# One attention and mixture-of-experts kernel, with the written order of its steps replaced

## The chip, the cores and the metric

The program runs on one core of a Trainium2 chip. The metric is device time in microseconds (us) of one execution. A core has TensorE (PE: matmuls, with its weight loads PEld), VectorE (DVE), ScalarE (ACT), GpSimdE (POOL) and SyncE (SP). SyncE issues nearly all DMA transfers of this kernel, one after the other, from one queue.

## The reference

```python
# clustered attention, 4 batches x 8 heads, 768 rows, 64 columns a head
q_assign = np.argmax(einsum(q_n, c_n)); k_assign = np.argmax(einsum(k_n, c_n))   # 16 clusters
mask = q_assign[:, :, :, None] == k_assign[:, :, None, :]
scores = np.where(mask, scale * q @ k.T, -1e9)
attn = softmax(scores); x = attn @ v                  # then heads side by side: (4, 768, 512)
# mixture of 4 experts over x, each a causal attention head of width 64
logits = x @ w_gate; topk = argpartition(-logits, 2)[..., :2]; w = softmax(selected logits)
for e in range(4):
    ye = softmax(causal(scale * (x @ wq[e]) @ (x @ wk[e]).T)) @ (x @ wv[e]) @ wo[e]
    out += (topk == e) * w * ye
```

## The kernel before, in words

The work is cut into 24 units: n = 0 to 15 are pairs of attention heads (called heads here), n = 16 to 23 are pairs of experts. The kernel first builds a plan: a list of 3726 steps (`op(...)`), each with an engine, a model duration, a function that issues its instructions, and the steps and buffers it depends on. Then `Plan.run` (line 278) walks a written list, `SEQ`, and calls the functions in that order. A token is the number of a step; a letter behind it (a, d, p) says that the step runs on its second engine (ScalarE, VectorE, GpSimdE). Each engine thus gets its own in-order queue, cut from this one list. `SLOT` says, also written out, which buffer of a tag (`ps` for the PSUM banks, `vt`, `acc`, `xt` and others) each tile takes. The durations in `op` are read by a planner that is not part of the kernel; the kernel runs the written order, whatever they say.

What one head does, with the lines that matter here:

- Its k, q and v are loaded (`load`, line 498, 384 KB each) and k and q transposed on TensorE (line 516). Clusters are found (lines 540 to 595), which gives `rows`, the one-hot rows of the mask.
- `place_rows` (line 598) sends `rows` into the operand tiles: tq<-rows and tk<-rows, 96 KB each. `put` (line 611) sends the high and low halves of k and q: tk<-hi, tk<-lo, tq<-hi, tq<-lo, each as two transfers of 192 KB. The steps of the first row of a head's maxima need `need_row` (rows, k high, q high), the scores need `need_st` (all).
- TensorE computes scores for the maxima (line 1055, 24 matmuls of 384 columns a head), VectorE reduces each (line 1061, then M at line 1065), TensorE transposes the maxima (line 1076), ScalarE or VectorE negates them into `mr`, and SyncE sends that 6 KB row into the operand tile (tq<-mr, line 1089).
- TensorE computes the scores again with the maximum row as an added term (lines 1134 and 1135, or the split pair 1138 and 1143), ScalarE takes the exponential (line 1153), and TensorE multiplies by v (line 1191). Line 1134 needs the operand halves and line 1135 also the row of maxima, tq<-mr. Both are one step, except in the first two blocks of a head, where they are two (1138, 1143).
- Row sums are added up over the blocks by `sum_op` (line 373): line 375 when GpSimdE runs it, line 376 when VectorE does. They go through TensorE (line 1215), DRAM (sd, r, rd) and a broadcast load (rb<-rd), and scale the result (line 1266), which is stored (x<-xt).

The experts project x (lines 773 and 813), take maxima and scores in the same way (lines 970, 978 and 1003) and multiply by wo (line 1305). All data are float32; "f32" and "fp32r" in the rows are two ways in which TensorE reads it.

The steps of SyncE that the prediction names: 658, 1208 and 1892 are the tq<-mr of heads 3, 6 and 10; 762 and 761 are tk<-rows and tq<-rows of head 4, 774 and 775 its tq<-hi; 580 is the v load of head 3; 1324 and 1325 are the tq<-hi of head 7, 1326 its tq<-lo, 1301 its v load; 736 is the x<-xt of head 3, 903 and 904 the rd<-r and rb<-rd of head 4; 1629 is the k load of head 9.

Of the kernel before, what the change touches and what calls it, by code (L numbers as in the profile page):

```python
# [42 lines left out]
163 164 148 149 256 257 152 153 134 120 121 112 113 254 131 258 260 423 122 123 168 169 124 125 135 116 117 137 150
151 166 161 162 146 411 167 118 147 251 566 138 139 155 156 132 128 171 133 129 140 412 413 126 127 119 141 154 159
172 160 176 165 259p 170 255p 175 142 143d 306 414 415 263 281 282 264 279 280 144 177 145 416 417 420 261 419 200
201 307 277 186 195 196 424 425 278 180 181 304 428 429 273 292 293 305 426 427p 187 191 192 283 284 267 268 430 432
431p 207 567 184 202 208 568 433 203 185 262 250 434 288 289 310 311 274 197 198 182 189 183 188 275 276 205 269 270
# [12 lines left out]
772 513 514 950 656 554 951 521 522 768d 774 769p 580 775 761 657d 658 707 814 687 688 505d 543d 510d 515d 773 776  # L60
388 389 390 221 548d 520d 553 815 955 956 804 805 948 952d 971 949p 674 957 958d 708 793 777 523 556 557d 960 555
675 524 908 558 672 673 794 778 816 817 810 806 811 781 751 1125 391 953p 392 665 822 823 818 559 973 972 961 682
683 666 667 791 659 660 661 779 807 819 783 784 792 780 782 824 962 963 964 662 684 663 685 664 1116 560 561 562 393
825 677 668 679 680 669 670 671 676d 795 678 681 789 790 689 797 798 690 692 808 809 720 693 796 686 691 820 821 965
966 812 722 723 702 703 696 697 787 967 968 970 813 785 799 800 786 788 801 802 803 826 700 701 712 713 698 699 704
710 978 974 975 717 718 721 979 1121 827 828d 829 976 980 982 983 969 981 977 984 715 716 705 706 830 711 725 709d
714 719d 724 1128 1129 1126 873 853 893 831 845 1127d 1122d 1117 1118d 874 854 832 860 861 846 694 695d 726d 727 921
728 1131 1132 894 564 1123 1124p 729 730 1119 1143 1287 563 565 1120p 1144 1142 991 987 988 858 859 1007 1008 992
1028 999 993 883 884 839 840 994 1026 841 1027 843 844 1014 1029 1010 1015 1011 1133 833 834 835 1018 1019 850 1032
851 1024 1025 1134 1135 731 732 959 733 1296 1000 1033 836 837 838 842 847 997 848 849 855 985 986 852 1030 1031 998  # L70
# [11 lines left out]
903 1325 1301 904 1629 1208 1103 1106 1107d 1355 1473 1474 1465 1466p 1461 1462p 1074d 1108 1485 1486 1484 911 1349  # L82
# [12 lines left out]
1544 1658 1659 1660d 1664 1666 1391 1392d 1667 1438 1439 1446 1802 1394 1413 1414 1397d 1665 1661 1668 1115 1283  # L95
# [111 lines left out]
    vt="010101010101111011100110010101",  # L207
    mx="0110011010100101010101011001100110101010",
# [1180 lines left out]
```

## Time and profile before

| what | value |
| --- | --- |
| median of 3 runs | 709.67 us |
| the runs | 711.19, 709.67, 703.8 us |
| the profiled execution | 703.06 us |
| its span, first to last instruction | 701.3 us |
| mean granted TensorE clock in it | 0.99 |
| data moved by DMA | 90.78 MB |

The profile is of one execution, the 703.06 us one. A row of a timeline gives start and length in us, the engine, the line, what is written and read, and in brackets how long the engine stood idle before and what ended that. Rows of SyncE are marked SPq and give the time of issuing, not of the transfer itself. PEclk is the granted share of TensorE's full clock.

### The profile page before, as it was taken

Reading aid. Unit: us, or ns where it says so; the run is one execution under the profiler, and the core shown is the slowest. Engines: PE = TensorE matmul, PEld = TensorE weight load, DVE = VectorE, ACT = ScalarE, POOL = GpSimd, SP = SyncE. Lnnn points to the kernel's source line nnn. Section 1 sums busy time; section 2 is a strip of 40 time slices with the busy share of each in tenths; the row PEclk is TensorE's granted clock in tenths of the full one; section 3 lists DMA queues with packets and bytes.
Section 4 is the critical chain, followed back from the end, with each engine's and each line's share of the span. In section 5 each row is a group of like instructions: output and inputs, shape, how many; then the busy total and the mean of one; then the engine's idle time right before and its main releaser. Section 6 shows DMA issues by size and latency. Waiting matters only on the chain.

```text
span 701.3 us, 13445 instructions
## 1 busy us (share of the span) xinstructions
PE 675.0 (96%) x4817; PEld 520.0 (74%) x4817; DVE 551.1 (79%) x1210; ACT 339.9 (48%) x787; POOL 332.5 (47%) x279
## 2 busy tenths in 40 slices
PE   8899997998988998999999999999999999999998
PEld 6778676676675775766776769787987988997766
DVE  5998986796969988999998987867677758968433
ACT  5646454465453663645664752355433334313623
POOL 6695654675834445717665742218503451404300
PEclk9999999999999999999999999999999999999999
DMA  7787567677765769565868435313022111021223
GB/s 223 170 184 171 126 173 171 171 178 148 209 160 130 184 183 219 129 191 142 194 159 222 124 93 122 92 47 92 2 68 72 48 50 61 24 100 56 76 94 121
DMA packets 70734, 90.78 MB, mean 129 GB/s; under 512 B 21088, under 2 KB 60428, under 8 KB 70668
## 3 DMA queue, kind: packets, MB, share of 16 engines
q1 hardware_dynamic: 70524, 89.90, 50.0%
q8 instruction: 38, 0.62, 0.4%
q14 instruction: 28, 0.23, 0.1%
q10 hardware_dynamic: 144, 0.03, 0.0%
HBM read 36.54 MB, written 12.91 MB: 71 GB/s over the span
## 4 chain that ended last, share of the span: by engine, by line
PE 53%; DVE 5%; DMA 3%; issue 2%; SPq 1%; ACT 1%; POOL 1%; DVEq 0%; ACTq 0%
PE banks L1191 10%; PE banks L773 9%; PE banks L1003 6%; PE banks L1305 5%; PE banks L813 5%; PE banks L1055 3%; PE banks L1134 3%; PE banks L1135 3%; PE banks L970 2%; PE banks L1215 2%; SPq L358 1%; DVE wvl L376 1%; PE banks L516 1%; DVE mx L1061 1%; POOL acc L375 1%
## 5 line engine op out<-in xcount | busy, mean ns | idle before, releaser
L1061 DVE TENSOR_REDUCE mx<-banks 128x1 f32<-128x384 f32 x384 | 191.6, 549 | 34.2 <-PE banks L1055 33.4
L1135 PE MATMUL banks<-tq,tk 97*128 97x384 f32 x324 | 111.4, 344 | 9.9 <-DMA tq<-mr 9.9
L1055 PE MATMUL banks<-tk,tq 80*128 80x384 f32 x384 | 112.0, 363 | 5.9 <-DMA tk<-rows 2.0
L1134 PE MATMUL banks<-tq,tk 128*128 128x384 f32 x324 | 115.3, 356 | 0.6 <-DVE mx L1061 0.6
L1055 PEld LDWEIGHTS banks<-tk,tq 80*128 80x128 f32 x384 | 69.1, 192 | 18.7 <-issue 11.6
L1153 ACT ACTIVATE p<-banks 128x384 f32<-128x384 f32 x144 | 66.6, 498 | 30.0 <-PE banks L1135 12.5
L1135 PEld LDWEIGHTS banks<-tq,tk 97*128 97x128 f32 x324 | 62.4, 193 | 11.2 <-DMA tq<-mr 11.2
L1134 PEld LDWEIGHTS banks<-tq,tk 128*128 128x128 f32 x324 | 62.1, 192 | 9.7 <-DVE mx L1061 3.2
L375 POOL TENSOR_TENSOR acc<-acc,p 128x768 f32<-128x768 f32 x21 | 39.7, 1890 | 46.8 <-DVE acc L376 44.6
L370 ACT ACTIVATE avu<-banks 128x384 f32<-128x384 f32 x31 | 15.2, 490 | 80.0 <-PE banks L1191 77.7
L978 DVE CUSTOM_DVE_ANT_0 banks<-banks,tri 128x384 f32<-128x384 f32 (+4 forms) x96 | 45.8, 528 | 7.8 <-PE banks L970 7.6
L1191 PE MATMUL banks<-p,vt 128*64 128x384 f32 x288 | 50.5, 490 | 0.0
L1153 ACT ACTIVATE xl<-banks 128x384 f32<-128x384 f32 x88 | 41.8, 497 | 14.0 <-PE banks L1135 13.3
L1153 ACT ACTIVATE xh<-banks 128x384 f32<-128x384 f32 x80 | 38.3, 499 | 16.7 <-PE banks L1135 15.7
L375 POOL TENSOR_TENSOR lo<-xk,hi 128x384 fp32r<-128x384 f32 x27 | 27.0, 1010 | 36.2 <-DVE mx L1061 12.7
L1003 PE MATMUL banks<-tk 64*128 64x384 f32 (+2 forms) x432 | 44.1, 313 | 0.0
L1191 PEld LDWEIGHTS banks<-p,vt 128*64 128x64 f32 x288 | 19.6, 137 | 24.2 <-issue 22.2
L1003 PEld LDWEIGHTS banks<-tk 64*128 64x128 f32 x432 | 34.8, 185 | 2.3 <-ACT tk L1017 0.5
L1191 PE MATMUL banks<-xl,vt 128*64 128x384 f32 x176 | 31.0, 489 | 0.0
L1266 POOL TENSOR_TENSOR xt<-avu,rb 128x384 f32<-128x384 f32 x26 | 27.2, 1055 | 7.5 <-DMA rb<-rd 6.7
L1017 ACT ACTIVATE tq<-banks 128x768 f32<-128x768 f32 (+2 forms) x41 | 26.8, 672 | 5.2 <-PE banks L1003 4.2
L1191 PE MATMUL banks<-xh,vt 128*64 128x384 f32 x160 | 28.2, 488 | 0.0
(316 smaller groups left out, 1692.6 us busy)
## 6 DMA issues: line engine op xcount, KB each, us to landing
tk<-hi SPq DMA_DIRECT2D x60, 192.0 KB
tq<-hi SPq DMA_DIRECT2D x56, 192.0 KB
rb<-rd SPq DMA_DIRECT2D x46, 192.0 KB
vt<-in_v_dram SPq DMA_DIRECT2D x16, 384.0 KB
x<-xt SPq DMA_DIRECT2D x16, 384.0 KB
kt<-in_k_dram SPq DMA_DIRECT2D x15, 384.0 KB
qt<-in_q_dram SPq DMA_DIRECT2D x15, 384.0 KB
tk<-lo SPq DMA_DIRECT2D x30, 192.0 KB
```

Of the source, the lines that this page charges most:

```text
L375: ways = [("pool", t_pool(n), lambda: POOL.tensor_tensor(dst(), a(), b(), op=fn)), ("dve", t_dve(n), lambda: DVE.tensor_tensor(dst(), a(), ...
L773: PE.matmul(m()[:, :HW], w_()[:, dc, es], x_[dc]()[:, js], start=(i == 0), stop=(i == 3 * DC - 1))
L813: PE.matmul(m()[:, :NV], x_[dc]()[:, ts], w_()[:, dc, :], start=(i == 0), stop=(i == 3 * DC - 1))
L978: DVE.tensor_tensor_reduce(ps()[:, h, :w], ps()[:, h, :w], tri[:, 512 - w:], 1.0, -3.0e38, OP.add, OP.max, to)
L1003: PE.matmul(p()[:, h, o_:HW], kone[0][r] if a is None else a()[r, ks], b()[r, qs], start=(j == 0), stop=(j == 3))
L1055: PE.matmul(ps()[:, :w], Q[0:R, 0, h, c * 128:(c + 1) * 128], K[0:R, 0, h, i * w:(i + 1) * w], start=True, stop=True)
L1061: DVE.tensor_reduce(mx()[:, h, cc, i:i + 1], ps()[:, :w], axis=AX.X, op=OP.max)
L1134: PE.matmul(p()[:, o_:HW], K[:, 1, h, ks], Q[:, 1, h, qs], start=True, stop=False)
L1135: PE.matmul(p()[:, o_:HW], K[0:R, 0, h, ks], Q[0:R, 0, h, qs], start=False, stop=True)
L1153: ACT.activation(pt()[:, h, po:po + w], p()[:, o_:HW], AF.Exp, scale=SC)
L1191: PE.matmul(av()[h * 64:(h + 1) * 64, o_:HW], d["vv"](h, kc), pt()[:, h, po:po + HW - o_], start=(kc == 0), stop=(kc == nk - 1), tile_posi ...
L1305: PE.matmul(m()[:, :n1 - n0], a_()[:, ts], w_()[:, ep, n0:n1], start=(ep == 0 and i == 0), stop=(ep == EP - 1 and i == 2))
```

## The change

The order `SEQ`, the engine letters in it and the buffer numbers `SLOT` are replaced. Steps, operations, tiles and buffers are the same 3726. The first heads follow an older order of theirs; all later steps follow an order made with a planner's model in which a transfer has an issue time, a flight time and a time for which it occupies the DMA engines, so that transfers queue one behind the other. These numbers are in the `op("sp", ...)` entries, which got a third figure. The diff, cut to the places around steps 658, 1208 and 1892 and to the changed entries:

```diff
@@ SEQ
...
-491 492 493 516 759 760 762 544 500 608 609 655 615 621 630 503 504 517 946 508 545 509 770 766 767 771 947 501 502
-772 513 514 950 656 554 951 521 522 768d 774 769p 580 775 761 657d 658 707 814 687 688 505d 543d 510d 515d 773 776
...
-1463 1364 1365 1206 1207 1366 1347 1367 1460 1468 1469 1339 1356 1340 1354 1357 1073 1464 1088 1093 1098 736 1326
-903 1325 1301 904 1629 1208 1103 1106 1107d 1355 1473 1474 1465 1466p 1461 1462p 1074d 1108 1485 1486 1484 911 1349
...
-1756d 1788 2147 2148 1789 2009 2007 1625 1890 1891 1457 2003 2029 2030 2050 2051 2143 2044 2144 2027 2028 2154 2021
-2010 1985 1892 2145 2149 2169 2152 2153 2155d 2031 2019 2020 2023 2046 2042 2043 1790 1757 1758 1791d 2157 2158 2024
...
+549 758 617 608 497 550 614 219 642 387 498 552 759 615 513 760 950 609 538 508 499 630 762 655 766 518 767 761 770
+656 946 771 657 509 658 554 768d 772 951 773 775 514 500d 519 505d 774 388 510 389 521 555d 769p 952 515 776 948d
...
+1318d 1199 1174 1177 1323p 1324 1104 1200 1192 1319p 1175 1325 1179 1083 902 1180 1198 1205 1464d 1088d 1105 1206
+1468 1207 1459 1093 1469 1208 1470 1460 1339 1374 1471d 1341 903 1329 1340 1358 1326 1473 1375 1070 1465 1342 1362
...
+1996 2009 1778 1767d 1772 1623 1624 1854 1849 1855 2007p 2003 2010 1774 1865 1779 1788 1789 1777d 1782d 1787 1755
+1756 1749 1754 1864 1866 2050 1889 1890 1891 1892 2051 2154 2155 2058 2059 1625 1626 2044 2029 2030 2048 2049 2045
...
@@ SLOT
...
-    vt="010101010101111011100110010101",
+    vt="001101010101101100011010101010",
-    acc="010101010101101010100101010101100101",
+    acc="010101010101010101010110101001101001",
...
@@ load
-            return t, op("sp", [(0.5, 4.5)], go, due, use=[t])
+            return t, op("sp", [(0.5, 2.8, 1.32)], go, due, use=[t])
@@ place_rows
-        need_row = [op("sp", [(0.6, 2.8)], place_rows(Q, 0), c2 + 8, [o_r] + free, [rows]),
+        need_row = [op("sp", [(0.6, 2.15, 0.84)], place_rows(Q, 0), c2 + 8, [o_r] + free, [rows]),
@@ put
-            return op("sp", len(pars) * [(0.65, 3.6)], go, due, after + free, use)
+            return op("sp", len(pars) * [(0.65, 2.3, 0.96)], go, due, after + free, use)
...
@@ core
-                o = op("sp", [(0.84, 1.2)], go, due + 0.5, [o] + (d["zero"] if moe else sets_free(n)), [mr, qm] if moe else [mr])
+                o = op("sp", [(0.84, 1.14, 0.04)], go, due + 0.5, [o] + (d["zero"] if moe else sets_free(n)), [mr, qm] if moe else [mr])
...
```

The number of steps on each engine, from the letters of the two lists: TensorE 1425 and 1425, SyncE 375 and 375, ScalarE 759 and 760, VectorE 915 and 871, GpSimdE 252 and 295. Of the 324 steps made by `sum_op`, 172 were on GpSimdE and 211 are now.

## Rows read from the trace of the kernel before

**Rows 1.** The page, part 1: engine busy us, share of the span, instructions.

```profile
PE 675.0 (96%) x4817; PEld 520.0 (74%) x4817; DVE 551.1 (79%) x1210; ACT 339.9 (48%) x787; POOL 332.5 (47%) x279
```

**Rows 2.** Busy us of each engine in two stretches, granted clock, DMA share, GB/s.

```profile
0.00:420.00 420.00, 397.48 (x2632) 288.84 (x2633) 358.52 (x716) 232.10 (x548) 247.64 (x191) 0.99 0.69 169
420.00:701.00 281.00, 277.54 (x2186) 231.11 (x2185) 192.56 (x495) 107.80 (x239) 84.86 (x89) 0.99 0.23 70
```

**Rows 3.** Who waited for whom, TensorE: us in total, times, longest.

```profile
PE banks L1135 <- DMA tq<-mr: 9.9, 5, 4.3
PE banks L1076 <- DVE M L1065: 2.3, 2, 2.0
PE banks L1055 <- DMA tk<-rows: 2.0, 1, 2.0
PE banks L1055 <- DMA tq<-rows: 2.0, 1, 2.0
```

**Rows 4.** Timeline of SyncE's queue, 100 to 105 us: start, us of issuing, transfer.

```profile
100.07 1.26 SPq L358 DMA_DIRECT2D tq<-hi  x2
101.38 0.59 SPq L358 DMA_DIRECT2D vt<-in_v_dram  x1
102.02 1.25 SPq L358 DMA_DIRECT2D tq<-hi  x2
103.31 0.60 SPq L358 DMA_DIRECT2D tq<-rows  x1
104.01 0.84 SPq L358 DMA_DIRECT2D tq<-mr  x1
```

**Rows 5.** Timeline of TensorE, 105 to 111 us.

```profile
105.39 0.45 PE L1134 MATMUL banks<-tq,tk 128*128 128x384 f32 x1
110.16 0.69 PE L1135 MATMUL banks<-tq,tk 97*128 97x384 f32 x1 [4.32 <-DMA tq<-mr]
```

**Rows 6.** Timeline of TensorE, three other waits for transfers.

```profile
198.77 0.60 PE L1135 MATMUL banks<-tq,tk 97*128 97x384 f32 x1 [3.28 <-DMA tq<-mr]
...
276.48 0.59 PE L1055 MATMUL banks<-tk,tq 80*128 80x384 f32 x2 [1.96 <-DMA tq<-rows]
...
309.15 0.44 PE L1135 MATMUL banks<-tq,tk 97*128 97x384 f32 x1 [1.21 <-DMA tq<-mr]
```

**Rows 7.** Timeline of SyncE's queue, the issues of those three transfers.

```profile
193.64 0.83 SPq L358 DMA_DIRECT2D tq<-mr  x1
...
270.94 0.60 SPq L358 DMA_DIRECT2D tq<-rows  x1
...
305.67 0.84 SPq L358 DMA_DIRECT2D tq<-mr  x1
```

**Rows 8.** Stretches around three waits, columns as in rows 2 (clock third from last).

```profile
110.16:113.56 3.40, 3.40 (x12) 3.21 (x13) 1.31 (x3) 1.15 (x3) 0.00 (x0) 0.50 0.31 87
113.56:117.00 3.44, 3.44 (x37) 2.43 (x36) 2.68 (x7) 2.41 (x7) 2.64 (x3) 1.00 0.93 261
198.90:202.30 3.40, 3.40 (x12) 3.31 (x13) 1.94 (x4) 0.49 (x1) 0.78 (x1) 0.50 0.97 248
277.40:280.80 3.40, 3.40 (x19) 2.34 (x21) 2.75 (x8) 1.25 (x3) 0.00 (x0) 0.50 0.36 100
```

**Rows 9.** Chain that ended last: start us, us, what (DMA from issue to landing).

```profile
249.54 1.27 PE banks L1055 x7
...
270.94 5.40 DMA tq<-rows
...
305.67 3.44 DMA tq<-mr
...
344.28 4.02 PE banks L1191 x24
```

**Rows 10.** Timelines of VectorE and GpSimdE, 407 to 409 us.

```profile
407.00 0.95 DVE L376 TENSOR_TENSOR xl<-vm,xh 128x768 fp32r<-128x768 f32 x1
...
408.72 1.73 DVE L376 TENSOR_TENSOR xl<-vm,xh 128x768 fp32r<-128x768 f32 x1
...
407.16 4.99 POOL L375 TENSOR_TENSOR acc<-acc,xl 128x768 f32<-128x768 f32 x2 [5.08 <-DVE acc L376]
```

More of the change, by code (lines that the diff above doesn't have):

```diff
@@ L43 @@
[L43 to L47, printed above, removed]
@@ L61 @@
[L61 to L65, printed above, removed]
@@ L66 @@
[L66 to L70, printed above, removed]
@@ new lines @@
+20 88 422 108 246 13 89 242 104 109 17 96 243 406 97 404 407 100 105 92 575 405 244 101 106 245 93 402p 409 111 247
+99 410 102 107 114 229 90 126 115 94 91 230p 249 86 256 95 148 252 87 168 149 163 103 421 169 157 110 257 164 152
+158 253 112 153 130 248 173 113 131 132 120 258 127 124 411 254 133 259p 128 166 260 129 155 167 125 146 398p 156
+118 412 161 147 136 226p 174 150 423 162 171 134 151 135 160 172 154 261 413 121 251 255p 137 116 414 138 304 415
+290 159 117 122 408 416 140 119 417 176 566 123 262 139 165 305 141 291 420 288 142 289 428 419 277 143 170 424 429
@@ new lines @@
+1116 520 522 957 972 822 947 787 958d 668 799 823 669 679 670 580 788 806 543 802 707 908 803 687 708 800 816 390
+659 680 810 817 660 688 665 949p 818 807 661 820 682 811 812 548 793 683 821 698 700 794 699 662 819 672 797 813 663
+673 666 553 798 717 667 804 808 701 791 805 684 718 792 795 664 955 953p 796 824 814 956 702 815 781 783 703 973 674
+782 785 809 677 779 825 678 392 960 1125 826 675 780 556 784 961 671 523 685 524d 777 557 689 778 789 558 962 690
+786 391 692 790 801 909 963 676 971 964 681 693 965 827 722 966 686 712 828d 967 829 710 968 705 696 711 969 978 706
@@ new lines @@
+833 974 979 723 559 720 975 715 970 721 867 976d 697 845 980d 716 836 855 868 704 982 837 848 560 838 878 846 856
+393 713 725 981p 983 879 709d 221 977 561 714 984 726d 834 871 835 691 1007 1117 849 1008 1028 1010 1118 839 869
+1011 872 840 562 1029 991 870 1018 719 830 841 992 995 891 1119 1019 1001 858 1002 850 859 996 1020 843 851 1021 993
+999 844 1126 994 892 860 724d 1127 831 853 832 1121 1000 1014 842 989 1122 1128 990 861 888 1296 854 1015 886 1129
+1024 1287 1123d 1003 1032 887 985 920 1124p 1030 1033 1131 1025 1142 847 1004 727 1132 694 1031 695 893 1143 889 987
@@ new lines @@
+873 988 1120p 1133 874 728d 1026 1005 1134 894 923 1012 852 863 729 1006 1144 1135 875 986 959 1027 857 1013 1136
+1022 997 1137 881 998 1138 730 883 1023 564 1139 1016 1009 876 1017 884 1292 1140 563 1034 1149 1145 1293 1141 1035
+1150 1036 882 1146 1037 877 896 1151d 1147 880d 864 1153 885d 731 1148p 1154 1152 1044 1051 890d 732 1041 1068 1052
+1155 1061 897d 895 1069 1288 1062 1045 1038 1289 1039 1130 1096 1046 1297 1040 1053 862 1097 733 1042 1294d 1189
+1290 1058 1190 1054 1077 1059 1075 1314 1172 1078 1193 1168 1043 1056 1194 1291p 1089 1173 1057 1458 1063 1090 1201
@@ new lines @@
+1635 1527 1531 1514 1241 1631 1509 1506 1528 1405 1109 1421 1507 1406 1301 1639 1515 1632 1383 1800 1384 1269 1532
+1422 1545 1380 1656 1640 1423 1546 1385 1504 1520 1518 1505 1386 1419 1521 907 1539 1381 1420 1519 1387 1398 1424
+1540 1400 1382 1274d 1395 1388 1431 1399 1529 1533 1432 1410 1530 1396 1389 1534 1512 1390 1428 1513 1391 1535 1393
+1411 1536 1392 1523 1543 1394 1110 1408 1429 1544 1541 1111 1409 1277 1655 1644 1278 1397 1401 1244 1645 1245d 1403
+910 1498 1510 1404 1525 1112 1637p 1646 1511 1524 1413 1526 1633p 1279 1647 1402 1809 921 1648 1657 1407 1499 1649
@@ new lines @@
+1697 1448 1690 1804p 1415 1815 1449d 1416 1283 1808p 1816 1701 1450 1564 1683 1684 1695 1575 1565 1568 1573 1284
+1285 1828 1827 1451 911 1980 1578 1583 1702 1685 1817 1818 1704 1679 1671 1705 1672 1819 1710 1711 1584 1585 1680
+1686 1703 1675 1594 1595 1596 1820 1821 1691 1692 1706 1714 1715 1698 1676 1699 1822 1823 1825 1824 1599 1600 1597
+1607 1687 1608 1598 1829 1830 1831 1832p 1708 1833 1834 1835 1837 1707 1452 1453 1838 1286 1673 1674 1688 1693 1614
+1712 1713 1709 1718 1604 1836 1601d 1605 1606d 1611 1612 1613 1615 1617 1618d 1616 1719 1720 1721 1983 1984 1858
@@ new lines @@
+1859 1887 1846 1875 1876 1856 1857 1847 1981 1982 1972 1973 1871 1869 1873 1872 1976 1852 1860 1870 1861 1888 1974
+1586 1977 1986 1978 1987 1454 1839 2142 1619 1456 1455 1998 1853 1979p 2151 1587d 1620d 1621 1997 1877 1878 1874
+1770 1771 1842 1740 1741 1752 1753 1883 1728 1768 1862 1863 1745 1769 1746 1881 1882 1844 1750 1751 1729 1730 1785
+1786 1884 1843 1879 1880 1840 1988 1731 1732 1841 1989 1990 1722 1723 1724 1742 1743 1733 1725 1726 1727 1759 1760
+1763 1764 1775 1737 1738 1747 1867 1735 1748 1736 1776 1975p 1999 1845 1991 1992 1850 1851 1868 1885 1761 1762 1622
@@ new lines @@
+2207 2225 2226 2485 2112 2113 2351 2327 1967 2352 926 2126 2208 2231 2196 2235 2194 2195 2197 2105 2106 2489 2101
+2102 2109 2398 2399 2115 2116 2388 2389 2206 2396 2397 2486d 2496 2497 2494 2495 2120 2353 2232 2233 2234 916 2121
+2130 2491 2487 2511 2510 2114d 930d 931 927 2119d 2124d 2129d 2490 2499 2500 912 928 2099 2657 2132 2133 2100 2134
+2156 2354 2131d 2386 2387 2236 2237 914 2296 2394 2395 2253 2400 929 2401 2501 2297 2263 2264 2248 2249 918d 2278
+2255 2241 2392 2256 2254 2250 2251 2279 2242 2666 2135 2488p 2492p 2512 2384 2244 2245 2246 2281 2282 933 936 2502
@@ new lines @@
+2775 2789 2780 2784 2785 2773 2778d 2783 2889 2890 2897 2881 2882 2978 2979 2799 2800 2843 2815 2810 2794 2795 2813
+2898 2845 2792 2793 2803 2808 2804 2483 2790 2791 3061 3062d 3063 2805 2899d 2797 2798 2802 2796d 2801d 2806 2807d
+2809 2811 2816 2814 2818 2786 2819 2787 2812d 2817d 2820 2821d 2974 2975 2968 2969 3064 3065 3066p 2951 2900 2921
+2922 2935 2936 2927 2928 2976 2977 2931 2932 2911 2912 2913 2972 2973 2905 2906 2907 2964 2965 3067 3068d 3069 2924
+2925 2919 2920 2970 2901 2966 2967 2902 2903 2971 2980 2873 3073 3074 3075 3079 2844 2653 2655 2822 2312 2823 2824
@@ new lines @@
+2981 2982 3076 3077d 3080 3081 3078 3070 3071d 3072 2983 3018 2933 2937 3019 3020 2994 2995 2996 2874 2654 2846p
+3110 3111 3002 3003 3104 3105 3010 3011 3116 3117 3007 3008 3004 3005 3102 3103 3014 3015 3016 2904 2929 2908 2909
+2988 2989 2990 2991 3114 3115 2923d 2926d 2984 3106 2985 2986 3281 2987 2825 3108 2826 3109 3181 3090 3091 3178 3182
+3179 2930d 2934d 2938d 3183 3180 3107 3172 3173 3174 3175 3176d 3177 2875 2910 2914d 3088 3089 3112 3113 3118 3190
+3186 2915 2941 2917 2916 2942 3084 3085 3119 3187 3082 3120d 2918d 2993 3086 3087 3083 3191 3092 3093 3198 3199 3192
@@ new lines @@
+3193 3006 3012 2992 3009 3013 3282 3283p 3121 3140 3141 3145 3146 3152 3153 3194 3195 3132 3133 3148 3149 3184 3185
+3196 3197 3200 3122 3123 3124 3284 3285d 3286p 3142 3143 3126 3188 3127 3128 3156 3157 2998 2939 2940 3022 3017 3021
+3024 2997 3000 3287 2656 3288d 3289 2876 2877 3278 3279d 3280 3299 3189 2828 2827d 3094 3025d 3201 3202 2999 3296
+3297d 3298 3095 3001 3290 3291d 3292 3096 2943 2944 2878 3203 2829 2879 2945 2946 3300 3023 2880 3501 3026 3293
+3294d 3295 3301 3304 3305 3326 3327 3222 3223 3330 3331 3204 3205 3206 3134 3144 3150 3147 3328 3329 3214 3215 3216
@@ new lines @@
+3224 3225 3334 3335 3230 3231 3322 3323 3227 3228 3336 3337 3208 3209 3210 3154 3211 3151d 3155 3238 3234 2947 3027
+2948 2949d 3207 3158 3332 3028 3333 3338 3159d 3239 3240 3029 3498 3324 3325 2950 3235 3236 3125 3129 3130d 3131d
+3135 3312 3313 3302 3392 3393d 3030 3031 3394 3306 3307 3308 3395 3396d 3401 3402 3397 3403 3032 3033 3398 3303 3399
+3400 3339 3310 3340 3341 3309 3138 3139d 3311 3499 3502 3162 3163d 3164 3416 3417 3213d 3412 3503p 3500p 3226 3212
+3232 3229 3410 3411 3160 3161d 3413 3136 3137 3414 3415 3360 3361 3404 3405 3362 3363 3352 3353 3418 3419 3376 3377
@@ new lines @@
+3372 3342 3373 3406 3407 3420 3233 3237 3365 3366 3346 3347 3348 3368 3507 3508 3369 3509 3408 3409 3241 3165 3504
+3505 3506p 3218 3219d 3314 3242 3097 3098 3099 3101 3038 3519 3520d 3521 3421 3513 3514 3515 3100 3166 3516 3517
+3315 3518 3422d 3423 3243d 3039 3040d 3510 3511d 3512 3217 3220 3167 3168 3244 3245d 3221 3343 3344 3542 3543 3548
+3549 3442 3443 3447 3448 3458 3459 3552 3553 3450 3451 3554 3555 3444 3445 3550 3551 3454 3455 3428 3429 3556 3557
+3430 3434 3435 3424 3425 3544 3545 3546 3370 3364 3367 3349 3169p 3316 3371d 3374 3375 3460 3431 3246 3041 3247 3248
@@ new lines @@
+3387 3388 3268 3432 3258 3259 3631 3640 3627 3641 3642 3532 3461d 3464 3465d 3433 3437 3440 3260d 3441d 3466 3269
+3643 3467 3533 3534 3589 3590 3535 3536 3356 3380 3584d 3357d 3381d 3389p 3438 3439 3592 3654 3655 3593 3594 3680
+3681 3656 3685 3686 3687 3676 3677 3261 3572 3596 3597 3321 3468 3469 3470 3682 3644 3645 3648 3649 3573 3598 3646
+3647 3650 3574 3651 3678 3566 3567 3568 3569 3570d 3585 3586 3672 3673 3571d 3575d 3587d 3591d 3595d 3599d 3669 3667
+3537 3538 3670 3274 3275 3262 3263 3276 3277 3668 3578 3602 3603d 3539 3579d 3604 3264 3265 3540 3462 3576 3675
@@ L193 @@
+3390d 3391 3474 3463d 3671d 3471 3472 3605 3473 3486 3487 3488d 3674d 3475 3476 3477 3489 3657 3600 3679d 3606 3683d
+3607 3608 3490 3491 3492 3601 3493 3577 3482 3483 3484 3485 3690 3652d 3692 3691 3653d 3660 3661 3659 3494 3495 3496
+3497 3478 3479 3480 3481 3609 3610 3662 3658d 3693 3663 3664 3611 3665 3666 3694 3684 3688 3689 3695 3696 3697 3706
+3707 3708 3709 3698 3699 3714 3715 3716 3717 3700 3701 3710 3711 3712 3713 3541 3702 3703 3704 3705 3718 3719 3720
+3721 3722 3723 3724 3725
 """
@@ L218 @@
-    ps2="31123232332231001223120300012121323203113023321103022032310322111213200032303023232010021301122331120010"
-        "32003130221303120110223003312221",
+    g="01320132",
+    ps2="32120331031231200011322313020302132310112102103223032131013300011012232210332021013033311322110332011200"
+        "31330222310333211200213011210120",
 )
@@ L602, in attention_operands @@
             free = [op("pool", 2.7, lambda: clear_rows(n % 3), t0 - 60)]
-        need_row = [op("sp", [(0.6, 2.8)], place_rows(Q, 0), c2 + 8, [o_r] + free, [rows]),
-                    op("sp", [(0.6, 2.8)], place_rows(K, 1), c2 + 8.2, [o_r] + free, [rows])]
+        need_row = [op("sp", [(0.6, 2.15, 0.84)], place_rows(Q, 0), c2 + 8, [o_r] + free, [rows]),
+                    op("sp", [(0.6, 2.15, 0.84)], place_rows(K, 1), c2 + 8.2, [o_r] + free, [rows])]
         need_row2, half_row = [], [need_row[:], need_row[:]]
@@ L669, in move @@
             def move(dst, src, due, after, use=()):
-                return op("sp", [(0.65, 2.2)], lambda: dma(dst, src()), due, after, use)
+                return op("sp", [(0.65, 2.1, 0.96)], lambda: dma(dst, src()), due, after, use)
             need_st += q_lo[::2] + [move(Q[high, 1, :, :HW], lambda: Q[low, 0, :, :HW], c2 + 14, need_row[-2:])]
@@ L1236, in go @@
                 dma(dr["s"][:, :, qd, :], ssb()[32 * qd:128:64])
-        o = op("sp", 2 * [(0.58, 1.7)], go, t1 + 7, sums, [ssb])
+        o = op("sp", 2 * [(0.58, 1.05, 0.04)], go, t1 + 7, sums, [ssb])
         r = tmp("r", (128, 12), bufs=2)
-        o = op("sp", [(0.37, 2.4)], lambda: dma(r(), dr["s"].rearrange("h f d j -> (h f d j)").rearrange("(p t) -> p t", t=12)),
+        o = op("sp", [(0.37, 1.2, 0.04)], lambda: dma(r(), dr["s"].rearrange("h f d j -> (h f d j)").rearrange("(p t) -> p t", t=12)),
                t1 + 9, [o], [r])
```

200 lines of the change are left out of this document (79 added, 121 removed), and 53 rows, old and new, of the table SEQ.

## The prediction

> **What bounds the kernel now.** I read the engine shares of the page first. TensorE shows 675.0 us of matmuls in a span of 701.3 us [rows 1], so whatever the new order gains has to come from the places where TensorE stands still or runs slowly. The two long stretches show where those are. In the first 420 us, the sixteen attention heads, TensorE is busy for 397.5 us, VectorE for 358.5 us, and the DMA engines for 0.69 of the time. In the remaining 281 us TensorE is busy for 277.5 us and DMA for only 0.23 [rows 2]. The second stretch is simply full of matmuls, and an order can't shorten it. The first has some 22 us of idle TensorE and a crowded DMA.
>
> The waits name the cause. Of the idle time before matmuls, 9.9 us in five waits is for the small transfer tq<-mr (the row of negated maxima, 6 KB) before line 1135, 2.0 us each is for tk<-rows and tq<-rows, and 2.3 us is for a VectorE reduction before line 1076 [rows 3]. A 6 KB transfer isn't slow by itself, so I looked at SyncE's queue ahead of the longest wait. From 100.07 to 104.01 us it issues four halves of tq<-hi (192 KB each), a v load (384 KB) and tq<-rows (96 KB), and only then tq<-mr [rows 4]: 4 x 192 + 384 + 96 = 1248 KB in front of 6 KB. The matmul that needs it starts at 110.16 us after 4.32 us of idling [rows 5], 6.1 us after the issue. The same shape stands before 198.77 us (idle 3.28), 276.48 us (1.96, on tq<-rows) and 309.15 us (1.21) [rows 6], whose transfers were issued at 193.64, 270.94 and 305.67 us [rows 7]. The planner's entry for this transfer was 0.84 us of issue and 1.2 us of flight, whatever lies ahead in the queue.
>
> A long wait costs a second time. From 110.16 to 113.56 us the granted clock is 0.50, the lower level (1.2 GHz), with 12 matmuls in 3.40 us against 37 in the next 3.44 us at 1.00. The same 3.40 us at 0.50 follow the waits that end at 198.9 and near 277 us [rows 8]. Each gives away 1.7 us.
>
> **The change part by part.** The edits to (issue, flight, occupancy) numbers alter nothing by themselves: the program runs the written order, and only the order, its engine letters and the buffer numbers reach the chip. All 375 SyncE steps, and all 1425 of TensorE, are the same in both. So matmul work is unchanged, and I cost three effects of the order.
>
> *Small transfers leave the crowd.* I counted, along each order, the matmul work between a transfer's place and its first user (0.18 us for a 384-column matmul, 4.0 us for a value product of six blocks, [rows 9]) and the KB issued within the 5 us ahead of it. For head 3's tq<-mr (step 658) it was 1248 KB ahead and 0 to 3.9 us of work behind; now it stands before steps 774 and 775 (the tq<-hi of head 4), with 580 KB ahead and 8.8 us behind. Head 6 (step 1208): from 2788 KB and 1.3 us to 768 KB and 2.0 us. Head 10 (step 1892): from 1920 KB and 2.4 us to nothing and 5.5 us. Head 10's last operand: from 2116 KB and 8.0 us to 576 KB and 5.6 us. Over stretches of 10 us of matmul work, six had transfers for over 300 GB/s in the old order and three have in the new. What goes, if these waits all go: 9.9 (tq<-mr) + 2.0 (tq<-rows) [rows 3] + 3 x 1.7 (clock, [rows 8]) = 17.0 us, and 1.0 of the 2.0 us on tk<-rows at the start, where the lead in the order rises from 0 to 3.5 us. Sum 18.0, bounds 12 and 20.
>
> *Other leads get shorter.* The new order starts some transfers just in time. tq<-mr of heads 4, 6 and 7 has 2.3, 2.0 and 1.5 us of work behind it with 512, 768 and 384 KB ahead. Landing took 3.44 us where 768 KB were just ahead (305.67, [rows 9]); by that I need 3.2, 3.4 and 3.0, short by 0.9, 1.4 and 1.5. Heads 13 and 14 have no work between place and user, but 4.9 to 5.2 us after the step that feeds them; SyncE often runs ahead of its place, so I take 1.5 for both together (bounds 0 and 9.4). Heads 1 and 2: 0.9. That is 6.2 us. For tq<-hi, the last operand before a head's maxima, the lead was mostly 8 to 9 us and is now 3.3 to 5.8 us in heads 1 to 10, 0.4 in head 15. A landing in the crowd took 5.40 us [rows 9] and the first half's issue 0.65 more; by that the shortfalls add up to 19.9 us at the short end of the leads and 7.8 at the long end (a 3.9 us value product may cover the place). In less crowded spots the old run did with about 4.5 us, which leaves 0 to 7.1 us; I take 1.5, near that lower row, because fewer KB now stand ahead. One wait of 2 us or more that drops the clock: 1.7. Coming back: 6.2 + 1.5 + 1.7 = 9.4, bounds 2 and 30.
>
> *Sums move from VectorE to GpSimdE.* VectorE steps fall from 915 to 871 and GpSimdE's rise from 252 to 295; 39 of these are net sums (line 376 to line 375). That takes some 40 us off VectorE in all, some 25 in the heads, where it is the second-fullest engine. TensorE waits 2.3 us for it before line 1076 [rows 3]; I take 1.0, bounds -4 and 4. If this cover fails, a GpSimdE sum of 1.8 us sits where a 0.95 us VectorE sum was, and the row sums of the head come later; nothing on TensorE's chain waits for these soon.
>
> At 407.00 us a VectorE sum takes 0.95 us and at 408.72 us the same sum takes 1.73, started while GpSimdE's pair of sums from 407.16 us ran [rows 10]. The Trainium skill (SBUF — State Buffer, "Who interferes with whom") says that a VectorE instruction with two SBUF inputs and a GpSimd instruction that reads SBUF exclude each other for a whole instruction, whichever starts first; the trace agrees, with 0.78 us added. By it more GpSimdE sums would slow the VectorE sums that remain.
>
> *The buffer numbers and the second stretch.* Which of a tag's buffers a tile takes changes everywhere, and with it what a step waits for; in the second stretch only 3.5 of 281 us are idle on TensorE [rows 2], so the most that this part can give is 3.5, and as it is reordered too it can lose as much. I take nothing for both.
>
> Sum: 18.0 + 1.0 - 9.4 = 9.6 us off the profiled execution's 703.06, or 693.5 us. The runs' median is 709.67, 6.6 above that execution. I read that spread as transfers that crowd differently from run to run; with fewer of them crowded I keep two thirds of it, 4.4 us, and forecast 698.0 us.
>
> **The rivals.** *Slower: the tight leads don't hold.* If every tq<-hi needs its crowded 6.05 us, the shortfall is 19.9 us in place of 1.5, and four waits (heads 3, 6, 9, 15) drop the clock in place of one: 5.1 us more. 693.5 + 18.4 + 5.1 = 717.0 in the terms of the profiled execution, 721.4 on the medians. For it speaks that leads fell to near half; against it that the KB issued ahead of a head's last operand in heads 1 to 10 were between 96 and 2896 and are between 576 and 1248, and that heads run at 4.5 to 5.5 us today without a wait. It decides against the change once the shortfall passes the 9.6 us gained.
>
> *No change: VectorE takes the place of the transfers.* VectorE is at 358.5 of 420 us [rows 2]. If TensorE, no longer held by transfers, is held by the maxima instead, only the clock's share comes back: 2 us, 701 and, with the full offset, 707.7. For it: the fullest stretches of VectorE; against it: its load falls.
>
> *No change: the exclusion of the sums.* If each of the 43 added GpSimdE steps held a VectorE sum for 0.78 us, VectorE would have 33.5 us more; with 61.5 us free in 420 [rows 2] I let a third of it reach TensorE, 11 us: 704.7, on the medians 709.1.
>
> **How the numbers follow.** The forecast has 0.60, VectorE's rival 0.19, the exclusion 0.05 and the tight leads 0.16. A measurement of this kernel can tell about 1% from no change. The forecast's case lies below 702.6, hence faster 0.60, same 0.24, slower 0.16. Low end: 18.0 + 4 gained and only 2 given back, 683, and a small offset, 685. High end: between forecast and the first rival, 714, where about a tenth is left above.
>
> **What would show it.** Right: the wait of line 1135 on tq<-mr falls from 9.9 to some 6 us or less, no wait of 3 us or more, one or no stretch at clock 0.50 in the heads, VectorE's busy time some 30 to 45 us lower, GpSimdE's some 50 to 80 higher, the second stretch unchanged. Wrong: waits of line 1055 on tq<-hi or tq<-rows in several heads (first rival), or unchanged attention time with waits on line 1061 (second).

## The result, and the profile after

The changed kernel takes 686.01 us (median of 4 runs, 683.79 to 688.21) where the kernel before took 706.73 us (median of its 4 runs). The ratio is 0.970, with a 95% interval of 0.963 to 0.977: faster by 3.0%. Medians here are over all runs; ratios and their intervals leave out runs more than 1.5% above the fastest of their kernel. I had forecast 698.0 us and faster; 686.0 lies in the range of 685 to 714, one us above its low end. The profiled execution of after took 683.79 us with a span of 681.9 us, that is 19.3 us less than the one of before.

The page, part 1, answers to [rows 1]:

```profile
PE 668.1 (98%) x4817; PEld 517.3 (76%) x4817; DVE 530.5 (78%) x1166; ACT 340.2 (50%) x788; POOL 391.7 (57%) x322
```

TensorE is idle for 681.9 - 668.1 = 13.8 us, where it was idle for 701.3 - 675.0 = 26.3. So 12.5 of the 19.4 us of span are idle time that went. The two stretches, as in [rows 2], show where:

```profile
0.00:420.00 420.00, 410.09 (x2747) 303.81 (x2748) 356.56 (x726) 235.39 (x558) 292.76 (x224) 1.00 0.70 176
420.00:682.00 262.00, 258.03 (x2072) 213.48 (x2071) 173.96 (x441) 104.83 (x230) 98.97 (x99) 0.99 0.20 64
```

In its first 420 us TensorE runs 2747 matmuls where it ran 2632. In the second stretch it is idle for 4.0 us, as before (3.5). The waits of TensorE, answering to [rows 3]:

```profile
PE banks L773 <- DVE mx L1061: 3.0, 1, 3.0
PE banks L1215 <- DVE acc L376: 2.4, 3, 1.5
PE banks L1215 <- DVE wvl L376: 1.4, 1, 1.4
PE banks L1321 <- DVE onesb L385: 1.1, 1, 1.1
PE banks L516 <- DMA kt<-in_k_dram: 1.0, 1, 1.0
```

The first row of before, 9.9 us on tq<-mr, has no successor: none of this view's rows names tq<-mr, tq<-rows, tk<-rows or tq<-hi. What is left at the top is VectorE's. The places where the clock fell answer to [rows 8]:

```profile
400.08:403.49 3.41, 3.19 (x10) 3.19 (x11) 2.56 (x7) 0.00 (x0) 1.51 (x2) 0.50 0.02 2
...
662.90:666.30 3.40, 3.40 (x9) 2.67 (x9) 1.43 (x7) 0.52 (x1) 0.00 (x0) 0.50 0.00 0
```

Of the three half-clock stretches in the heads none is left. One new one follows the 3.0 us wait on VectorE; the one near the end stood at 676.8 us in before too. In the new order's two later profiles the same wait was 1.4 and 3.0 us, with a stretch at 0.50 behind it each time.

### The profile page after: what moved, and what is told of

It is laid out like the page before. It is cut to its first block, busy times and chain, and to the rows that moved or that the text cites. A ratio compares the mean times of both kernels' runs of the same rounds, so it can differ in the third digit from the quotient of the medians.

```text
span 681.9 us, 13437 instructions
## 1 busy us (share of the span) xinstructions
PE 668.1 (98%) x4817; PEld 517.3 (76%) x4817; DVE 530.5 (78%) x1166; ACT 340.2 (50%) x788; POOL 391.7 (57%) x322
## 5 line engine op out<-in xcount | busy, mean ns | idle before, releaser
L1134 PE MATMUL banks<-tq,tk 128*128 128x384 f32 x324 | 113.9, 352 | 0.0
L1135 PE MATMUL banks<-tq,tk 97*128 97x384 f32 x324 | 109.8, 339 | 0.0
L375 POOL TENSOR_TENSOR acc<-acc,p 128x768 f32<-128x768 f32 (+1 forms) x26 | 45.8, 1763 | 28.8 <-DVE acc L376 27.4
L375 POOL TENSOR_TENSOR acc<-p,p 128x768 f32<-128x768 f32 x9 | 16.6, 1845 | 48.7 <-ACT p L1153 29.8
L1191 PEld LDWEIGHTS banks<-p,vt 128*64 128x64 f32 x288 | 19.4, 136 | 24.0 <-issue 20.5
L375 POOL TENSOR_TENSOR lo<-xk,hi 128x384 fp32r<-128x384 f32 x29 | 30.6, 1068 | 10.2 <-DMA tq<-lo 8.3
L1266 POOL TENSOR_TENSOR xt<-avu,rb 128x384 f32<-128x384 f32 x30 | 31.5, 1060 | 8.0 <-DMA rb<-rd 6.9
```

Source lines behind the costliest of these rows:

```text
L375: ways = [("pool", t_pool(n), lambda: POOL.tensor_tensor(dst(), a(), b(), op=fn)), ("dve", t_dve(n), lambda: DVE.tensor_tensor(dst(), a(), ...
L1134: PE.matmul(p()[:, o_:HW], K[:, 1, h, ks], Q[:, 1, h, qs], start=True, stop=False)
L1135: PE.matmul(p()[:, o_:HW], K[0:R, 0, h, ks], Q[0:R, 0, h, qs], start=False, stop=True)
L1191: PE.matmul(av()[h * 64:(h + 1) * 64, o_:HW], d["vv"](h, kc), pt()[:, h, po:po + HW - o_], start=(kc == 0), stop=(kc == nk - 1), tile_posi ...
```

## Why the tight leads hold

My fear was rows of maxima that are sent just in time. The tightest is head 7's. SyncE's queue in after, 199 to 206 us:

```profile
199.22 1.31 SPq L358 DMA_DIRECT2D tq<-hi  x2
203.90 0.83 SPq L358 DMA_DIRECT2D tq<-mr  x1
204.78 1.27 SPq L358 DMA_DIRECT2D tq<-lo  x2
```

And TensorE at the first matmul that uses it:

```profile
205.98 0.41 PE L1135 MATMUL banks<-tq,tk 97*128 97x384 f32 x1
```

Line 1135 starts 2.08 us after the issue, with no wait in brackets. SyncE had issued nothing between 200.53 and 203.90 us, and the next bulk transfer goes behind the row, not ahead of it. Head 6 is the same, with 768 KB of tq<-hi in the 5 us ahead of its row and a pause of 2.3 us between them:

```profile
174.42 2.60 SPq L358 DMA_DIRECT2D tq<-hi  x4
179.34 0.85 SPq L358 DMA_DIRECT2D tq<-mr  x1
```

```profile
181.82 0.34 PE L1135 MATMUL banks<-tq,tk 97*128 97x384 f32 x1
```

That is 2.48 us from issue to use, without a wait. In before the row of head 6 was issued at 193.64 us and waited for until 198.77, 5.13 us later [rows 6, 7]. SyncE's queue just ahead of it, in before:

```profile
188.94 1.56 SPq L358 DMA_DIRECT2D tq<-hi  x2
190.60 0.54 SPq L358 DMA_DIRECT2D vt<-in_v_dram  x1
...
192.96 0.58 SPq L358 DMA_DIRECT2D kt<-in_k_dram  x1
```

There the k load, 384 KB, is issued 0.1 us ahead of the row, with hardly a pause since the others. The bytes issued in the last 5 us are thus the wrong count: in after 384 and 768 KB of tq<-hi are among them, but they were issued before the pause. What the pauses did is in the DMA engines' share (the last column but one; it can read a little above 1). In after, behind the rows of heads 6 and 7:

```profile
180.00:182.00 2.00, 2.00 (x15) 1.11 (x14) 2.00 (x5) 0.65 (x2) 2.00 (x2) 1.00 0.06 6
204.00:206.00 2.00, 2.00 (x16) 1.82 (x14) 1.90 (x5) 1.99 (x5) 2.00 (x2) 1.00 0.01 3
```

In before, behind the row of head 6:

```profile
194.00:196.00 2.00, 1.49 (x15) 0.55 (x7) 1.97 (x6) 1.16 (x3) 0.21 (x1) 1.00 0.82 209
```

The rows of heads 6 and 7 had the DMA engines nearly to themselves. The Trainium skill (SBUF — State Buffer, "The DMA setup-cost knee") gives a transfer about 2 us that don't depend on its size; the 2.08 us from issue to use, within which head 7's row landed, agree.

## The experiments

Every kernel here computes the whole result.

**The old order with eight transfer moves** (waits of line 1135 undone where they stood):

```diff
-516 759 760 762 544 ... 769p 580 775 761 657d 658 ... 1325 1301 904 1629 1208 ... 1985 1892
+516 759 760 762 761 544 ... 769p 657d 658 774 775 ... 580 ... 1325 904 1208 1301 1629 ... 1892 1985
```

(also 1824 forward and 1296, a q load, back)

> The old order and the old engines, with the places of SyncE's transfers changed around five waits and nothing else: the rows of maxima of heads 3, 6 and 10 go ahead of bulk transfers that stood just before them, a q load goes behind the row of head 5, and the mask rows of heads 4 and 10 (tq<-rows) go to where they are ready. Theory (small transfers stuck behind bulk ones): the waits of 4.32, 3.28, 1.21, 0.9 and 1.96 us shrink to under 1 us each and at least two of the three stretches at clock 0.50 vanish, so 9 to 16 us less than before (ratio 0.977 to 0.987). Rival (the gain of the new order came from moving sums to GpSimdE): within 3 us of before. Rival (the waits just move to the next transfer, tq<-hi of the next head): within 4 us of before, with waits of line 1055 on tq<-hi of 2 us or more.

Measured: 712.34 us, ratio 0.9999 [0.9954, 1.0045]. TensorE's waits there:

```profile
PE banks L516 <- DMA qt<-in_q_dram: 5.9, 1, 5.9
...
PE banks L1135 <- DMA tq<-mr: 1.3, 2, 0.8
```

The 9.9 us on tq<-mr fell to 1.3, as wanted, but the q load that I had moved back came 5.9 us late itself. The experiment was spoilt by that move.

**The same without the q load's move:**

> The old order with the moves of the first experiment, but the q load (step 1296) left in its place, so that no bulk load comes late. Theory A (waits on the row of maxima behind bulk transfers, and their half-clock stretches, are most of the gain): line 1135 waits under 2 us in all on tq<-mr, no line-516 wait on a q load, and 8 to 13 us less than the kernel before: ratio 0.982 to 0.989, near 700 us. Theory B (the gain is spread over the whole order and a wait taken away only moves the idle time to the next late thing): ratio 0.993 or above although the waits on tq<-mr are gone.

Measured: 706.25 us against 711.27, ratio 0.991 [0.987, 0.995]: 5 to 6 us, between the two theories.

```profile
PE banks L1055 <- DMA tq<-rows: 4.2, 1, 4.2
PE banks L1055 <- DMA tk<-rows: 2.6, 1, 2.6
...
PE banks L1135 <- DMA tq<-mr: 1.3, 2, 0.9
```

The stretches at the lower level:

```profile
23.80:34.05 10.25, 10.25 (x44) 8.06 (x45) 6.34 (x15) 2.69 (x6) 6.14 (x8) 0.50 0.70 173
...
382.20:392.45 10.25, 9.52 (x49) 6.96 (x50) 4.79 (x10) 3.74 (x10) 1.96 (x2) 0.50 0.46 115
```

8.3 us of waits on tq<-mr before line 1135 went (9.9 less 1.3, and 0.3 that stand before line 1143). But TensorE, now earlier, stood 4.16 us for tq<-rows before a matmul at 382.94 us; in the kernel before it stood 1.64 us at the same place, and went on at 382.67 us. It had come there 2.25 us earlier and left 0.27 us later, and the next 10.25 us ran at 0.50, which is 5.1 us lost. The first stretch, at 23.80 us, costs as much. It follows the wait for tk<-rows, at a place that no move touched; in before's profile that wait was 2.0 us, with no stretch behind it. So this one profile, which is slower than before's, doesn't show the gain that the times show. What it does show is that freeing seven transfers isn't the change: another transfer was late next, and the new order has no wait on that one.

**The new order with bulk transfers put ahead of five rows of maxima:**

```diff
-439 315 ... 487 ... 829 ... 1469 1208 ... 1516 1379
+439 236 746 315 ... 605 751 487 ... 393 221 829 ... 1469 1326 565 1208 ... 1516 1497 1301 907 1379
```

> The new order and engines, with two or three bulk transfers (384 KB each, ready by then) put straight ahead of the row of maxima of heads 1, 2, 4, 6 and 7, which have 1.9 to 2.8 us from issue to user. Theory: each row lands 2 to 3 us later, waits of line 1135 or 1143 on tq<-mr of about 2 to 3 us come back in most of the five, and one to three stretches at clock 0.50 follow: 10 to 18 us more than the new order's 684 to 688 us, that is 695 to 705 us. Rival (sums on GpSimdE are the gain): at most 3 us more, under 691.

Measured: 694.49 us, ratio to the kernel before 0.977 [0.972, 0.981]. The new order wasn't timed beside it; in its three comparisons its medians were 685.2 to 686.0 us, 8.5 to 9.3 less, just under the 10 that I had expected at least. Of the waits

```profile
PE banks L1135 <- DMA tq<-mr: 8.1, 5, 2.6
```

this row is back. Four of the five are where loads had been put ahead, heads 1, 2, 6 and 7 (2.58, 0.95, 1.59 and 1.48 us); head 4's row, moved like them, isn't waited for. The fifth, 1.51 us at 319.62, is head 11's, where nothing was moved. The chain that ended last holds these transfers, head 11's the last:

```profile
55.24 5.09 DMA tq<-mr
84.54 3.26 DMA tq<-mr
186.75 4.19 DMA tq<-mr
213.14 3.68 DMA tq<-mr
...
313.22 6.36 DMA tq<-mr
```

With the loads right ahead a 6 KB row lands after 3.26 to 5.09 us. The KB don't fix the time: heads 1 and 2 both have 768 KB straight ahead, and took 5.09 and 3.26. Head 11's 6.36 us says more on pauses: SyncE issued nothing between 305.21 and 308.60 us, and yet the DMA engines stayed full:

```profile
306.00:308.00 2.00, 2.00 (x14) 1.96 (x13) 1.78 (x6) 2.00 (x7) 1.31 (x1) 1.00 1.07 214
```

So a pause by itself isn't enough. Another 960 KB stood straight ahead of this row too; how much of the 6.36 us comes from either wasn't separated. The place behind the bulk transfers is therefore a cause, shown from both sides. It is worth 5 to 9 us in these two experiments; how the rest of the new order's gain divides among its other moves, its letters and its buffer numbers wasn't measured.

**Order and engine letters exchanged.** The new order with the old letters (266 steps differ), and the reverse:

> The new order, with every step on the engine on which the old order had it (266 letters differ; 39 sums net go back to VectorE). Theory (transfers are the gain, VectorE is a cover): 2 to 8 us more than the new order, 688 to 695 us, with waits on VectorE and none on tq<-mr. Rival (the engines are the gain): 12 us more or above, 698 us or more.

> The old order, with every step on the engine on which the new order has it. Theory: the waits on tq<-mr stay (about 10 us in total before line 1135), so within 5 us of before either way, ratio 0.993 to 1.007. Rival (the engines are the gain): 10 us or more less than before, ratio under 0.986.

Measured: 793.35 us (ratio 1.116 [1.111, 1.121]) and 825.28 (1.159 [1.154, 1.165]). Neither expectation had the size, and the second not even the sign. The longest waits of the second are

```profile
PE banks L1076 <- DVE M L1065: 12.5, 3, 6.5
PE banks L1055 <- DVE mx L1061: 9.6, 3, 5.4
```

An engine takes its steps in the order of the list, so a step on another engine's queue stands in front of other steps than the order was made for. Order and letters can't be priced apart.

**43 of the moved sums back on VectorE** (beside a run of the new order, 685.19 us, ratio to the kernel before 0.964, as expected). The edit drops the letter that puts a sum on GpSimdE or adds the one for VectorE, at the same places:

```diff
-... 598p 459 333d 338 ... 515 776 ... 543 802 ... 676 971
+... 598 459 333d 338 ... 515d 776 ... 543d 802 ... 676d 971
```

> The new order with every second one of the 86 sums that had gone from VectorE to GpSimdE put back on VectorE, at the same places of the list: 43 sums, 66 us less on GpSimdE by their durations in the new order's profile, some 40 us more on VectorE, 29 of them in the heads. If the move of the sums was worth little by itself, as my term of 1.0 us with bounds of -4 and 4 says, the time stays within 4 us of the new order (ratio to it 0.994 to 1.006). If the order needs these sums on GpSimdE, since VectorE is nearly full in the heads and its sums stand in front of maxima, it is 8 us or more slower, with waits for VectorE (lines 1055, 1076 and 1215) over 6 us in all.

> The changed kernel once more, as the yardstick of this batch: 683 to 688 us, a ratio of 0.962 to 0.974 to the kernel before.

Measured: 722.17 us, slower than the kernel before (1.017 [1.012, 1.022]) and 37.3 us [34.8, 39.8] slower than the new order. Its waits:

```profile
PE banks L1055 <- DVE mx L1061: 7.1, 4, 5.3
...
PE banks L578 <- DVE oh L567: 3.9, 4, 2.8
PE banks L1076 <- DVE M L1065: 3.8, 3, 2.3
```

VectorE isn't full (557.7 of 720 us) and has as many instructions as in the kernel before (1209 and 1210), but a sum in its queue stands in front of maxima and of the cluster steps (line 567), and TensorE waits for those. The 37.3 us are thus what these letters cost in an order made for others, not what moving the sums gained.

**Keeping the sums of the two engines apart.** The 3.0 us wait in after is made by rows like these. VectorE in after:

```profile
392.50 0.55 DVE L371 CAST xh<-vm 128x768 fp32r<-128x768 f32 x1
393.08 2.46 DVE L376 TENSOR_TENSOR xl<-vm,xh 128x768 fp32r<-128x768 f32 x1
395.46 1.36 DVE L371 CAST xh<-vm 128x768 fp32r<-128x768 f32 x1
396.75 2.16 DVE L376 TENSOR_TENSOR lo<-xq,hi 128x384 fp32r<-128x384 f32 x1
398.83 0.94 DVE L376 TENSOR_TENSOR xl<-vm,xh 128x768 fp32r<-128x768 f32 x1
399.70 2.40 DVE L1061 TENSOR_REDUCE mx<-banks 128x1 f32<-128x384 f32 x5
```

and GpSimdE beside it:

```profile
392.69 2.03 POOL L375 TENSOR_TENSOR acc<-acc,p 128x768 f32<-128x768 f32 x1
394.95 1.46 POOL L1266 TENSOR_TENSOR xt<-avu,rb 128x384 f32<-128x384 f32 x1 [0.23 <-DMA rb<-rd]
396.37 2.12 POOL L375 TENSOR_TENSOR acc<-acc,p 128x768 f32<-128x768 f32 x1
```

The same VectorE sum took 0.95 us at 407.00 in before [rows 10]. Each of the three VectorE rows from 393.08 us ends 0.4 to 0.8 us behind the end of a GpSimdE row, about its own usual length. The maxima that TensorE needs stand behind them:

```profile
400.30 0.69 PE L773 MATMUL banks<-xh,wqh 128*128 128x384 f32 x1 [2.95 <-DVE mx L1061]
```

I took such meetings away in three steps, the first two beside a run of the new order (685.16 us, ratio to the kernel before 0.965, as expected). Not only places change: the second step puts one more step (940) on GpSimdE, the third puts two of the sums and three splits on VectorE.

```diff
@@ first step, at 400 us
-2837d 2693 2838 2740 ... 2478 2743 2855 2736 2737 2594 2310 2600 2848 2605d 2311 2689p 2695
+2837d 2838 2740 ... 2478 2743 2693 2855 2736 2737 2310 2848 2311 2689p 2594 2600 2605d 2695
@@ second step, also at 331 and 357 us
-2135 2488p 2492p 2512 ... 913p 1968 ... 943 937 938p 944p ... 942p 2661p 2411 2137 2138 915p ... 940
+2135 913p 2488p 2492p 2512 ... 1968 ... 943 937 ... 940p 2661p 2411 2137 2138 915p 938p 944p 942p
@@ third step, in place of some of these
-2743 2693 2855 2736 2737 2310 2848 2311 2689p 2594 2600 2605d ... 915p 938p 944p 942p
+2743 2594d 2600d 2855 2736 2737 2605d 2693 2310 2848 2311 2689p ... 943 937 917 938 944 942 ... 915p
```

> The changed kernel itself, once more, beside the others of this batch. Both theories expect what it gave before: a ratio of 0.965 to 0.976 to the kernel before, an execution of 683 to 690 us. If it comes out at 0.98 or above, the first comparison was lucky and the effect is nearer my forecast of 0.987.

> The new order with four places changed at 390 to 400 us: two GpSimdE sums of head 14 (2594, 2600) go behind the two scalings xt<-avu,rb and the low half of q, with VectorE's next sum (2605) after them, and VectorE's low half of q (2693) goes behind the maxima. If the late maxima there come from VectorE sums held by GpSimdE sums, the 2.95 us wait of line 773 falls under 0.8 us, xl<-vm,xh there takes 0.95 us in place of 2.46, the half-clock stretch at 400 us goes (1.7 us): 3 to 4.5 us less than the new order, ratio to it 0.9935 to 0.9955. If the maxima were late for another reason (the queue order on VectorE, the number of blocks), the wait stays over 1.5 us and the time within 1 us of the new order.

> As the one before, and also: the two low halves of k of head 14 go behind a weight split that waits for its cast (so they miss VectorE's three sums at 331 us), and five GpSimdE steps near 357 us go behind one that waits for a cast at 363.6 us (so they miss VectorE's five sums there). If the exclusion of the sums is the cause, the waits of line 1215 of 1.39 us (335 us) and 1.50 us (362 us) also go: 5.5 to 7.5 us less than the new order, about 677 us, ratio to the kernel before near 0.961. If not, no better than the run before it.

Measured: 684.21 us for the first step and 682.27 for the second, 0.9 us [-1.7, 3.5] and 2.6 us [0.1, 5.2] less than the new order beside them; less than expected. The profile of the second tells why (its line numbers are one higher). ScalarE, then TensorE:

```profile
405.01 0.49 ACT L1154 ACTIVATE p<-banks 128x384 f32<-128x384 f32 x1 [3.96 <-POOL acc L376]
```

```profile
405.55 0.45 PE L774 MATMUL banks<-xh,wkh 128*128 128x384 f32 x1 [2.05 <-ACT p L1154]
```

The delayed sum still held the tile p that the next exponential writes, and TensorE wanted the bank that this exponential empties. The wait was moved, not removed, and its half-clock stretch came with it. I put down another wait of 1.1 us to splits that I had set ahead of head 13's sums.

> The experiment of the three places, with its two side effects taken out: the sums 2594 and 2600 of head 14 run on VectorE behind the maxima, so that the exponential of line 1153 no longer waits for a GpSimdE sum, and the three weight splits near 357 us run on VectorE behind its sums, out of the way of head 13's sums on GpSimdE. In the profile of the three places TensorE waited 2.05 us for that exponential and 1.11 us for another, and ran one 3.4 us stretch at half clock behind the first (1.7 us). If these are the side effects, all three go: 4.9 us less than the profiled execution there, 4 to 7 us less than the new order on the medians, 678 to 681 us. If new waits take their place, it stays within 2.5 us of the new order, as the three places did.

Measured: 678.34 us (677.82 to 680.53), ratio to the kernel before 0.956 [0.952, 0.960], and 6.0 us [3.9, 8.1] less than the new order beside it. As expected, and better than both kernels. VectorE there:

```profile
391.71 0.96 DVE L376 TENSOR_TENSOR xl<-vm,xh 128x768 fp32r<-128x768 f32 x1
392.58 0.55 DVE L371 CAST xh<-vm 128x768 fp32r<-128x768 f32 x1
393.17 0.96 DVE L376 TENSOR_TENSOR xl<-vm,xh 128x768 fp32r<-128x768 f32 x1
```

GpSimdE has no instruction there between 391.2 and 393.7 us. TensorE's longest wait is 1.1 us, at the start, and no stretch of the heads is at 0.50. So the exclusion of the two engines' sums is shown by the rows, and the edits that avoid it are worth about 6 us together. What the changed places and letters gave besides wasn't separated.

## Why the prediction was right, and where its numbers were off

*What bounds the kernel.* Right: the idle time of TensorE in the heads went, the second stretch stayed.

*Small transfers leave the crowd: 18.0 us.* Right. All 9.9 + 2.0 + 2.0 us of waits and the three half-clock stretches in the heads (5.1) are gone, 19.0 us.

*Coming back: 9.4 us.* This is the step that failed, by its size. Of the 6.2 us for tq<-mr and the 1.5 us for tq<-hi nothing came; a k load at the start came 1.0 us late. The rule "Landing took 3.44 us where 768 KB were just ahead ... by that I need 3.2, 3.4 and 3.0" counted transfers that had all but left the DMA engines by then. Head 6 did with 2.48 us and head 7 with 2.08; in the experiment that put loads directly ahead, rows took 3.26 us and more. The 1.7 us for one clock drop came, but behind a wait on VectorE.

*Sums move: 1.0 us gained, bounds -4 and 4.* Wrong in sign, within the bounds. All rows of the waits view whose releaser is VectorE add up to 6.5 us in before and 8.6 in after, and one drop of 1.7 hangs on them. The wait for M (2.3 us [rows 3]) went; the waits for late sums and for the maxima behind them came. "Nothing on TensorE's chain waits for these soon" was false: line 1215 waited for sums, and line 773 for maxima behind them. And a term of its own this never was: order and letters belong together.

*The balance.* Idle time fell by 12.5 us: 13.9 on transfers and 1.6 on issue went, 1.0 for a k load and 2.1 on VectorE came, 0.1 is left over. And two half-clock stretches fewer (four to two) are 3.4 us. The other 3.5 us of the span are shorter busy time of TensorE beside that; which matmuls, and why, stays open. The new order's other two profiles have TensorE busy for 671.5 and 670.8 us, so executions of one kernel differ by as much.

*Luck.* The two profiles are 19.3 us apart, and the sum said 9.6. In its terms: 19.0 for 18.0, 1.0 given back for 9.4, 3.8 lost to VectorE (2.1 and one clock drop) where 1.0 was to be gained, and 5.2 that no term had (1.6 on issue, 3.5 of busy time, 0.1). The second error and the third pull in opposite directions. Without the loss to VectorE, which I had not foreseen, the time would have come out below my range, as that of the kernel of the third step did. That 686.0 is in the range owes something to this.

*Offset of the median.* I kept 4.4 us; it was 2.2. I had read the spread of the runs as transfers that crowd differently. What the runs show of it is time at the lower clock. For each run, span times (1 - mean granted clock) is the time lost to the lower level. In the 13 runs of the kernel before beside the first experiments (704.58 to 715.14 us) it goes from 7.0 to 17.1 us, nearly the whole spread; its mean is 13.8. The 16 runs of the new order in three comparisons (681.0 to 688.2 us) lose 2.0 to 5.5 us, 3.5 in the mean. So some 10 of the 25 us between these runs are clock, more than the 3.4 us between the two profiles, because before's profile is of one of its fastest executions. What made TensorE stand in the slower ones wasn't profiled. It can't be the rows of maxima alone: with seven transfers moved, the runs of the old order that its ratio counts still went from 697.1 to 707.1 us.

*Rivals.* The tight leads held; what would have broken them is now known (transfers directly ahead). VectorE in the place of the transfers came in part: 2.1 us and a drop. The exclusion of the sums, to which I gave 11 us and a chance of 0.05, was there, with some 6 us to be had from edits against it, beside the forecast's gain and not in its place.

*What would show it.* tq<-mr, the clock, the second stretch and GpSimdE (59.2 us more) came as written; "no wait of 3 us or more" held barely, at 2.95 us. VectorE's busy time fell by 20.6 us, not by 30 to 45. A sum that is held counts as busy, 2.46 us in place of 0.95. Over line 376 the mean rose from 0.94 to 1.01 us, which with 113 instructions left there is some 9 us; the rest isn't traced.

## What to carry to other kernels

Price a small transfer by what the DMA engines still have to move when it is issued, not by the bytes of a window: look for a pause of the queue ahead of it, and at the DMA share in that pause. When the transfers no longer hold TensorE, look at sums of VectorE and GpSimdE that start within each other's time. Put GpSimdE's beside VectorE's maxima, which read PSUM (all 384 took 0.49 to 0.56 us in after), and see which tile a delayed sum keeps. An order and the choice of engines in it are one decision; neither can be carried to the other's list.

## What was not expected of the hardware

A cast with one SBUF input was held too: 1.36 us in after, 0.55 with GpSimdE out of its way. The Trainium skill (SBUF — State Buffer, "Who interferes with whom") counts casts among the operations that can take the port pair shared with GpSimd; the trace agrees.

The length of a wait alone doesn't say whether the clock falls. In the experiment with bulk transfers ahead, TensorE waited 1.59 us before 190.98 us and 1.48 us before 216.86 us; the stretches behind them:

```profile
191.00:194.40 3.40, 3.40 (x20) 3.37 (x21) 2.04 (x5) 2.90 (x8) 2.13 (x3) 1.00 0.58 140
217.20:220.60 3.40, 3.40 (x13) 3.31 (x12) 0.56 (x1) 2.20 (x5) 0.90 (x1) 0.50 0.34 73
```

The longer wait left the clock at its upper level, the shorter was followed by 3.4 us at the lower.
